# PSUM banks handed out one by one, and in-weight conversions moved behind batch 0, in a fused attention and MoE kernel

## The chip, the cores and the metric

The kernel runs on one core of a Trainium2 chip. The metric is the device time of one launch in microseconds (us). The core's engines are PE (TensorE, the matrix engine), DVE (VectorE), ACT (ScalarE), POOL (GpSimd) and SP (SyncE), which here only issues transfers (DMA). Each engine works through its own instructions in order. PSUM, the memory that PE writes, has eight banks of 512 floats for each of 128 partitions.

## The reference, cut to what matters

Attention with a band below the row's maximum, for 8 batches, 8 heads, 576 tokens, head size 64; then a gated two-layer unit on the 4608 tokens of width 512, with an inner width of 1536:

```python
scores = scale * np.matmul(q, k.transpose(0, 1, 3, 2))
thresh = np.max(scores, axis=-1, keepdims=True) - tau
scores = np.where(scores >= thresh, scores, -1000000000.0)
attn = np.exp(scores - np.max(scores, axis=-1, keepdims=True))
attn = attn / (np.sum(attn, axis=-1, keepdims=True) + 1e-09)
x = np.matmul(attn, v)          # heads side by side: 4608 x 512
gate = 1.0 / (1.0 + np.exp(-(x @ w_gate)))
out = (gate * (x @ w_val)) @ w_out
```

The weights come in as 64-bit floats, which the kernel receives as pairs of 32-bit words.

## The kernel before, in words

**Attention** goes by *visits*: one batch and one pair of heads, 32 visits in all, four to a batch. A visit has nine score tiles: four of each head (128 queries against all 576 keys), and one of the leftover 64 queries of both heads. A score tile `s` takes two PSUM banks. PE fills it (lines 591 for the first four visits, 599 later); DVE takes each row's maximum (606); POOL or DVE works out the threshold (615); ACT takes the exponential into `p` (620); DVE masks and sums it (623), and with that the score tile is free. DVE inverts the sum (655), POOL scales `p` by it (657), PE transposes it in four pieces into one bank, `tp` (668), ACT copies that to `pt` (630); the leftover keys go the same way, `lk` to `pl` (681). Two tiles of both heads are then multiplied with the values into one bank, `av` (704), and ACT copies the result to `xf`. For the first blocks `xf` is split into a high and a low float half, `x` (714 on ACT, 716 on POOL).

**The MoE** follows batch by batch. A *unit* of the in-product is 12 matmuls of 512 columns into one bank `m` (764): 24 units to a batch (12 column blocks, gate and value), then the out-product `o` (807). The last six batches and the leftover tokens go in pairs through seven products instead of eight (1006 and 1071), with sums of weights worked out earlier on POOL.

**The weights** have to be converted from 64-bit floats once. A conversion loads the raw words (`wr`), takes an exponent part on POOL (424, `wa`) and ACT (428, `wb`, which holds a PSUM bank), joins words on DVE (431, 437), and makes a high half on ACT (449) and a low half on POOL (455) or DVE (451) into `ws`. `ws` is stored to DRAM (`wid` for gate and value, `wod` for out) and loaded again by later batches. The first `OWN` in-weights are also used by batch 0 from where they are made; the other in-weights batch 0 loads back (`wi_6_0a` and so on).

**What sets the order.** The program first lists all operations with their engine, a cost, a key and their dependences. A planner then plays them through in time: whenever an engine is free it starts the operation with the lowest key whose inputs are ready and whose buffers have room, and this order is what is issued. Keys are counted in score tiles: visit after visit takes nine. MoE matmuls have keys above all others on PE, so they fill what attention leaves. `CONV_IN` and `CONV_OUT` give the key of the first conversion and the step to the next; `SHIFT` is the gap between the keys of batch 0 and batch 1; `LAG` is what the planner allows between an operation's end and the start of one that depends on it on another engine; `SLOTS` counts the buffers of each kind. PSUM is two score tiles (tag `s`) and four single banks (tag `b`), each tag a pool that gives its buffers in turn. Of the four banks conversions may hold one, attention three (two once the MoE has begun), the MoE two, and all four after the last attention output.

## Time and profile before

| | |
|---|---|
| median of 3 runs | 1355.14 us (1352.18 to 1357.49) |
| span of the profiled execution | 1352.1 us, no time of its own is given beside it |
| PE / DVE / ACT / POOL busy | 98 / 71 / 54 / 47% |
| mean granted PE clock | 0.992 |
| moved by DMA | 317.83 MB, mean 235 GB/s |

The profile is of one execution. A row of a group reads: line, engine, operation, written and read tiles with shapes, count, then busy time and mean nanoseconds of one, then the engine's idle time just before those instructions and what ended it. A row of the waits reads: who waited for whom, us in total, times, the longest. A row of a timeline: start, duration, engine, line. "PEld" is PE's weight loads, "PEclk" the granted clock.

The page's row of 40 equal slices shows PE at 7 to 8 tenths in the first three slices (of 33.8 us) and at 9 or more from then to the last but one.

### The profile page before, as it was taken

What the parts mean: (1) busy time and instruction counts of PE and PEld (TensorE: products, weight loads), DVE (VectorE), ACT (ScalarE), POOL (GpSimd) and SP (SyncE); (2) the same over time, 40 slices, a digit from 0 to 9 for tenths busy, and PEclk for the clock granted to TensorE, in tenths of its full rate; (3) what the DMA queues carried; (4) which work ended last, traced back from release to release, by engine and by line L of the source; (5) the groups of instructions that cost most, each with busy time, mean ns of one, the idle gap of its engine ahead of it and who ended that gap; (6) DMA issues with size and microseconds to landing.
All of it is one profiled execution on the core that took longest, in us unless ns stands there. A gap on an engine that the chain in (4) does not pass through costs nothing.

```text
span 1352.1 us, 23686 instructions
## 1 busy us (share of the span) xinstructions
PE 1320.8 (98%) x8292; PEld 1084.1 (80%) x8292; DVE 954.8 (71%) x1943; ACT 726.9 (54%) x1339; POOL 630.3 (47%) x660
## 2 busy tenths in 40 slices
PE   7879999999999999999999999999999999999998
PEld 4557888888888888888888878888888888888887
DVE  7889868567877777778787763556965569654594
ACT  7878766666766766667776653223532225322242
POOL 6985957956777764967776741101000110001100
PEclk8989999999999999999999999999999999999999
DMA  9879999897978988898897858656695656756564
GB/s 341 279 251 309 311 257 269 233 279 209 264 212 242 261 242 227 250 267 238 238 270 188 241 179 295 205 180 211 201 308 183 201 193 204 249 180 204 186 221 129
DMA packets 140436, 317.83 MB, mean 235 GB/s; under 512 B 22048, under 2 KB 49952, under 8 KB 140320
## 3 DMA queue, kind: packets, MB, share of 16 engines
q1 hardware_dynamic: 140176, 316.33, 76.5%
q8 instruction: 67, 1.10, 0.4%
q14 instruction: 49, 0.40, 0.1%
q10 hardware_dynamic: 144, 0.00, 0.0%
HBM read 210.37 MB, written 54.53 MB: 196 GB/s over the span
## 4 chain that ended last, share of the span: by engine, by line
PE 87%; DMA 6%; DVE 2%; ACT 2%; issue 1%; POOL 1%; SPq 1%; ACTq 0%; DVEq 0%; POOLq 0%
PE m L764 13%; PE qb L1006 11%; PE av L704 11%; PE s L599 8%; PE qc L1006 7%; PE qa L1006 7%; PE tp L668 7%; PE o L807 6%; PE rb L1071 5%; PE rc L1071 4%; PE ra L1071 4%; DMA wo<-wod 2%; DMA kd<-k 2%; PE s_l L599 1%; PE lk L681 1%
## 5 line engine op out<-in xcount | busy, mean ns | idle before, releaser
L657 POOL TENSOR_SCALAR p<-p,zero_t,sm 128x576 f32<-128x576 f32 x256 | 216.3, 856 | 107.9 <-DVE sm L655 76.5
L606 DVE TENSOR_REDUCE st<-s 128x1 f32<-128x576 f32 x256 | 192.3, 754 | 91.9 <-PE s L599 83.2
L623 DVE SCALAR_TENSOR_TENSOR p<-s,st,p 128x576 f32<-128x576 f32 x256 | 205.9, 812 | 30.2 <-ACT p L620 23.9
L620 ACT ACTIVATE p<-s,st 128x576 f32<-128x576 f32 x256 | 190.2, 750 | 57.4 <-DVE st L606 56.5
L919 POOL TENSOR_TENSOR gA<-gA 128x512 f32<-128x512 f32 x18 | 24.1, 1341 | 416.2 <-DVE gA L985 416.2
L630 ACT COPY pt<-tp 128x512 f32<-128x512 f32 x256 | 147.4, 589 | 54.0 <-PE tp L668 51.9
L599 PE MATMUL s<-kd,qd 128*128 128x288 f32 x896 | 165.0, 308 | 3.7 <-issue 1.6
L668 PE MATMUL tp<-ident,p 128*128 128x128 f32 x1024 | 156.7, 282 | 2.5 <-POOL p L657 2.0
L764 PE MATMUL m<-x,wi 128*128 128x512 f32 x576 | 158.9, 403 | 0.0
L668 PEld LDWEIGHTS tp<-ident,p 128*128 128x128 f32 x1024 | 123.2, 143 | 29.4 <-POOL p L657 7.6
L599 PEld LDWEIGHTS s<-kd,qd 128*128 128x128 f32 x896 | 133.9, 190 | 14.6 <-DVE p_l L623 2.4
L704 PE MATMUL av<-pt,vs 128*64 128x256 f32 x1024 | 126.1, 389 | 0.0
L807 PE MATMUL o<-g,wo 128*128 128x512 f32 x432 | 117.5, 401 | 0.0
L943 DVE TENSOR_TENSOR qu<-qb,qp 128x512 f32<-128x512 f32 x72 | 49.8, 692 | 89.9 <-PE qb L1006 77.1
L764 PEld LDWEIGHTS m<-x,wi 128*128 128x128 f32 x576 | 99.9, 189 | 14.3
L1006 PE MATMUL qa<-xs_p,wa 128*128 128x512 f32 x432 | 109.6, 389 | 0.0
L704 PEld LDWEIGHTS av<-pt,vs 128*64 128x64 f32 x1024 | 68.6, 138 | 48.5 <-issue 7.5
L1006 PEld LDWEIGHTS qa<-xs_p,wa 128*128 128x128 f32 x432 | 81.1, 188 | 16.8
L807 PEld LDWEIGHTS o<-g,wo 128*128 128x128 f32 x432 | 75.5, 189 | 10.9
L630 ACT COPY xf<-av 128x256 f32<-128x256 f32 x64 | 25.6, 399 | 77.4 <-PE av L704 73.1
L911 ACT CAST gs_p<-gA 128x512 fp32r<-128x512 f32 x54 | 32.4, 620 | 64.5 <-DVE gA L985 26.5
L981 ACT ACTIVATE gA<-qa 128x512 f32<-128x512 f32 x18 | 10.8, 598 | 103.4 <-PE qa L1006 103.4
(148 smaller groups left out, 2628.3 us busy)
## 6 DMA issues: line engine op xcount, KB each, us to landing
kd<-k SPq DMA_DIRECT2D x112, 320.0 KB, 6.0
wi<-wid SPq DMA_DIRECT2D x48, 512.0 KB, 6.9
wo<-wod SPq DMA_DIRECT2D x36, 512.0 KB, 7.0
wa<-wid SPq DMA_DIRECT2D x36, 512.0 KB, 4.1
ws<-sid SPq DMA_DIRECT2D x36, 512.0 KB, 4.5
wt<-sid SPq DMA_DIRECT2D x36, 512.0 KB, 3.3
wo_p<-sod SPq DMA_DIRECT2D x36, 512.0 KB, 4.6
qd<-q SPq DMA_DIRECT2D x112, 128.0 KB, 4.6
```

Source lines behind the costliest of these rows:

```text
L599: nc.tensor.matmul(s.ap[:, c, :HALF], st(), mv(slice(kc + c * HALF, kc + (c + 1) * HALF)), start=m == 0, stop=m == len(steps) - 1,)
L606: op("DVE", 0.76, key, lambda: nc.vector.tensor_reduce(out=st.ap[:, 0:1], in_=sv(), axis=AX.XY, op=ALU.max, negate=True), reads=[s], write ...
L620: op("ACT", 0.74, key, lambda: nc.scalar.activation(p(), sv(), AF.Exp, bias=st.ap[:, 0:1], scale=1.0), reads=[s, (st, 0)], writes=[(g.p, i)])
L623: op("DVE", 0.9, key, lambda: nc.vector.scalar_tensor_tensor(out=p(), in0=sv(), scalar=st.ap[:, 1:2], in1=p(), op0=ALU.is_ge, op1=ALU.mult ...
L630: return op("ACT", act(n), key, lambda: nc.scalar.copy(dst(), src.ap), reads=[src], writes=[part])
L657: op("POOL", 0.9, key, lambda i=i: nc.gpsimd.tensor_scalar(out=p.ap[:, i * S : (i + 1) * S], in0=p.ap[:, i * S : (i + 1) * S], scalar1=zer ...
L668: nc.tensor.matmul(tp.ap[:, c, :], self.p.ap[:, o + c * P : o + (c + 1) * P], ident, is_transpose=True, start=c == 0, stop=c == NJ - 1, sk ...
L704: nc.tensor.matmul(av.ap[h * D : (h + 1) * D, a:z], vis.vs.ap[:, j, h], m(h), start=i == 0, stop=i == len(ms) - 1, skip_group_check=True,)
L764: nc.tensor.matmul(m.ap, wv[:, a, c * P : (c + 1) * P], xs[c].ap[:, z, c0:c1], start=e == 0, stop=e == 11,)
L807: nc.tensor.matmul(acc.ap, wv[:, f, a], g[fg * ND + f].ap[:, z], start=(fg, f, a, z) == (0, 0, 0, 0), stop=(fg, f, a, z) == (NFG - 1, ND - ...
L1006: nc.tensor.matmul(acc.ap, wv[:, y, (2 * h + c) * P : (2 * h + c + 1) * P], xt[prod][c].get()[:, z], start=e == 0 and prod in FIRST, stop= ...
L1071: nc.tensor.matmul(acc.ap, w.ap[:, e, c, y], gt[prod][2 * g + c].get()[:, z], start=m == 0 and g == 0 and prod in FIRST, stop=m == 5 and g ...
```

## The change

PSUM is no longer two rotating pools. For each `s` and `b` tile the planner now settles a *place* when the tile is given out: score tiles may take banks 0-1, 2-3 and, until the first MoE product is issued, 4-5; single banks are 6 and 7, and after that point also 4 and 5. Each place is a pool of its own with one buffer, so a tile waits only for the last user of its banks. Ahead of the first product there are thus three score tiles, and two banks for all else. With it go other numbers: in-conversions start at key 36 with a step of 2 (from 10 and 1.5), which is behind batch 0's attention; `OWN` is 24, so batch 0 loads no in-weight back; batch 1's keys start 35 behind batch 0 (50 before); POOL works out the thresholds of the first visit of batch 1 too; six low halves go from DVE to POOL; PE's lag is 1.0 instead of 1.2; there is one more buffer of `p`, `x` and `w`; and a visit's scores may not start before a given MoE unit has ended (three units to a visit, from the sixth visit on).

```diff
     def make(self, b):
+        if b.place is not None:
+            at = min(b.place)
+            tag = f"{b.tag}{at}"
+            return self.bank_pool(tag).tile(b.shape, b.dtype, tag=tag, name=b.name, bufs=1)
         pool, bufs = self.pools[b.tag]
...
+        if not self.settle([b for s in need.values() for b in s]):
+            return False
...
+    def settle(self, bufs):
+        taken = set().union(*self.live.values()) if self.live else set()
+        places = {}
+        for b in bufs:
+            if b.tag not in ("s", "b"):
+                continue
+            for at in self.homes(b.tag):
+                if not taken & at:
+                    places[b] = at
+                    taken |= at
+                    break
+            else:
+                return False
...
-    "p": 3, "pc": 1, "sm": 8, "st": 16, "pt": 2, "pl": 2, "ptc": 1, "plc": 1, "xf": 2, "x": 5, "g": 12,
-    "w": 8, "t2": 6,
+    "p": 4, "pc": 1, "sm": 8, "st": 16, "pt": 2, "pl": 2, "ptc": 1, "plc": 1, "xf": 2, "x": 6, "g": 12,
+    "w": 9, "t2": 6,
-CONV_IN, CONV_OUT = (10, 1.5), (56, 3)
+CONV_IN, CONV_OUT = (36, 2), (56, 3)
-THR_FIRST, THR_UNTIL, LK_UNTIL = "POOL", 36, 300
+THR_FIRST, THR_UNTIL, LK_UNTIL = "POOL", 72, 300
-OWN = 12
-SHIFT = 50
+OWN = 24
+SHIFT = 35
-DVE_LO_IN, DVE_LO_OUT = range(18,24), ()
-LAG = {"PE": 1.2, "DVE": 0.3, "ACT": 0.08, "POOL": 0.3, "SP": 0.08}
+DVE_LO_IN, DVE_LO_OUT = (), ()
+LAG = {"PE": 1.0, "DVE": 0.3, "ACT": 0.08, "POOL": 0.3, "SP": 0.08}
+RATE, SLACK = 3, 3
...
-    pools["s"], pools["b"] = (ps, 2), (ps, 4)
+    pools["s"], pools["b"] = (ps, 3), (ps, 4)
...
         def cap(self, tag, cls):
+            if tag == "s" and active["moe"]:
+                return 2 if cls is None else None
...
+        def homes(self, tag):
+            if tag == "s":
+                return [{0, 1}, {2, 3}] + ([] if active["moe"] else [{4, 5}])
+            return [{6}, {7}] + ([{4}, {5}] if active["moe"] else [])
...
+    def held_by(vis):
+        n = RATE * (4 * vis.b + vis.hp - 4) - SLACK
+        return [unit_ends[n]] if RATE and 0 <= n < len(unit_ends) else []
...
-    nc = _bacc.Bacc("TRN2", target_bir_lowering=False, num_devices=1)
+    nc = _bacc.Bacc("TRN2", target_bir_lowering=False, num_devices=1, dynamic_dma_scratch_size=2048)
```

How instructions move, at three places. Line numbers of the changed program are larger (591 is 638 there, 606 is 653, 623 is 670, 431 is 478, 437 is 484, 668 is 719). In names such as `s_0_020` the first number is the visit's pair, then the head and tile; `l` is the tile of the leftover queries.

PE at the start of the program, before:

```order
L591 MATMUL s_0_000_196<-kp_0_0_174,qp_0_176 128x288 x2
L591 MATMUL s_0_001_204<-kp_0_0_174,qp_0_176 128x288 x2
L591 MATMUL s_0_l_228<-kp_0_0_174,qp_0_176 64x288 x2
L591 MATMUL s_0_l_228<-kp_0_1_180,qp_0_176 64x288 x2
L591 MATMUL s_0_020_235<-kp_0_0_174,qp_0_176 128x288 x2
L668 MATMUL tp_0_000_251<-ident,p_0_00_215 128x128 x4
```

and in the change:

```order
L638 MATMUL s_0_000_199<-kp_0_0_177,qp_0_179 128x288 x2
L638 MATMUL s_0_001_205<-kp_0_0_177,qp_0_179 128x288 x2
L638 MATMUL s_0_020_214<-kp_0_0_177,qp_0_179 128x288 x2
L638 MATMUL s_0_l_241<-kp_0_0_177,qp_0_179 64x288 x2
L638 MATMUL s_0_l_241<-kp_0_1_183,qp_0_179 64x288 x2
L638 MATMUL s_0_021_248<-kp_0_0_177,qp_0_179 128x288 x2
L638 MATMUL s_0_100_258<-kp_0_1_183,qp_0_179 128x288 x2
L719 MATMUL tp_0_000_269<-ident,p_0_00_219 128x128 x4
```

Six score tiles now stand ahead of the first transpose, where four did.

DVE in the second visit of batch 0, before:

```order
L606 TENSOR_REDUCE st_1_100_595<-s_1_100_582 128x1
L623 SCALAR_TENSOR_TENSOR p_1_02_536,sm_1_02_552<-s_1_021_569,st_1_021_588,p_1_02_536 128x576
L655 RECIPROCAL sm_1_02_552<-sm_1_02_552 128x2
L623 SCALAR_TENSOR_TENSOR p_1_10_614,sm_1_10_626<-s_1_100_582,st_1_100_595,p_1_10_614 128x576
L606 TENSOR_REDUCE st_1_101_632<-s_1_101_618 128x1
L431 SCALAR_TENSOR_TENSOR wb_0_624<-wb_0_624,wa_0_478 128x512
L606 TENSOR_REDUCE st_1_120_644<-s_1_120_629 128x1
L437 SCALAR_TENSOR_TENSOR wa_0_478<-wr_0_362,wb_0_624 128x512
L623 SCALAR_TENSOR_TENSOR p_1_10_614,sm_1_10_626<-s_1_101_618,st_1_101_632,p_1_10_614 128x576
```

and in the change, from the same tile on:

```order
L653 TENSOR_REDUCE st_1_100_519<-s_1_100_487 128x1
L653 TENSOR_REDUCE st_1_101_527<-s_1_101_500 128x1
L653 TENSOR_REDUCE st_1_120_555<-s_1_120_521 128x1
L670 SCALAR_TENSOR_TENSOR p_1_10_529,sm_1_10_560<-s_1_100_487,st_1_100_519,p_1_10_529 128x576
L670 SCALAR_TENSOR_TENSOR p_1_10_529,sm_1_10_560<-s_1_101_500,st_1_101_527,p_1_10_529 128x576
L706 RECIPROCAL sm_1_10_560<-sm_1_10_560 128x2
L670 SCALAR_TENSOR_TENSOR p_1_12_563,sm_1_12_574<-s_1_120_521,st_1_120_555,p_1_12_563 128x576
L653 TENSOR_REDUCE st_1_121_587<-s_1_121_567 128x1
L484 SCALAR_TENSOR_TENSOR wa_1_351<-wr_1_208,wb_1_471 128x512
```

Three maxima now follow one another, and fewer conversion steps (431 and 437, now 478 and 484) stand between: up to the last masked sum of batch 0 there are 7 pairs of them where there were 18.

SP around the store that ends batch 0's last visit (`xp_3`), before:

```order
L460 DMA wid_1_120<-ws_1_1398 128x1024
L1177 DMA xp_3_139<-xf_3_1325 256x1x32
L535 DMA kd_1_0_1434<-k_1_1357 64x2x640 x2
L531 DMA qd_1_1_1441<-q_1_1385 64x512 x2
L416 DMA wr_2_1453<-in_moe_w_out_dram 128x1024
L535 DMA kd_1_1_1462<-k_1_1357 64x2x640 x2
L504 DMA kn_2_1472<-in_k_dram 128x640
L498 DMA vs_2_1477<-in_v_dram 128x768
L460 DMA wid_0_121<-ws_0_1460 128x1024
```

and in the change:

```order
L1228 DMA xp_3_142<-xf_3_1243 256x1x32
L578 DMA qd_1_1_1314<-q_1_1264 64x512
L582 DMA kd_1_1_1347<-k_1_1233 64x2x640
L507 DMA wid_1_113<-ws_1_1312 128x1024
L582 DMA kd_1_1_1347<-k_1_1233 64x2x640
L557 DMA qn_2_1360<-in_q_dram 128x640
L545 DMA vs_2_1366<-in_v_dram 128x768
L463 DMA wr_2_1371<-in_moe_w_out_dram 128x1024
L461 DMA wr_0_1402<-in_moe_w_gate_dram 128x1024
L507 DMA wid_0_114<-ws_0_1394 128x1024
L511 DMA wod_128<-ws_2_1404 512x1x256
L463 DMA wr_2_1490<-in_moe_w_out_dram 128x1024
```

Behind batch 0 SP now still has raw in-weights (`in_moe_w_gate_dram`, `in_moe_w_val_dram`) to load between those of the next visits; before, they had been issued by then. The twelve reloads of in-weights for batch 0 (`wi_6_0a` to `wi_11_1a`) are gone from SP's order further on. On every engine the other counts are as before, but for 10 copies of leftover keys (DVE to ACT) and 9 thresholds (DVE to POOL).

More of the change, by code (lines that the diff above doesn't have):

```diff
@@ L29, in __init__ @@
         self.plan, self.tag, self.shape, self.dtype, self.name, self.cls = plan, tag, shape, dtype, name, cls
-        self.t, self.accesses, self.users, self.held = None, [], 0, False
+        self.t, self.accesses, self.users, self.held, self.place = None, [], 0, False, None
         self.turn = plan.made[tag] = plan.made.get(tag, 0) + 1
@@ L52, in __init__ @@
         self.ops, self.held, self.made, self.given = [], {}, {}, {}
+        self.live = {}
     def buf(self, tag, shape, dtype, name, cls=None):
@@ L117, in cap @@
         return None
+    def settle(self, bufs):
[11 more added lines that the diff above has]
+                return False
+        for b, at in places.items():
+            b.place = self.live[b] = at
+        return True
     def run(self):
@@ L179, in run @@
                         if not b.users and b.held:
+                            self.live.pop(b, None)
                             self.held[b.tag] -= 1
@@ L353 @@
     nc.vector.tensor_scalar(out=scale_t, in0=tau_t, scalar1=0.0, scalar2=QSCALE, op0=ALU.is_ge, op1=ALU.mult)
-    warm = ps.tile([P, 2, SM], F32, tag="s", name="warm")
+    ahead = ExitStack()
+    ps_more = ahead.enter_context(tc.tile_pool(name="ps_more", bufs=1, space=PSUM))
+    warm = ps.tile([P, 2, SM], F32, tag="s0", name="warm", bufs=1)
     for i in range(WARM):
@@ L375, in cap, with bank_pool @@
             return 2 if active["att"] else 4
+        def homes(self, tag):
+            if tag == "s":
+                return [{0, 1}, {2, 3}] + ([] if active["moe"] else [{4, 5}])
+            return [{6}, {7}] + ([{4}, {5}] if active["moe"] else [])
+        def bank_pool(self, tag):
+            if tag == "s4":
+                return more[0]
+            if tag in ("b4", "b5"):
+                if more[0] is ps_more:
+                    ahead.close()
+                    more[0] = ctx.enter_context(tc.tile_pool(name="ps_late", bufs=1, space=PSUM))
+                return more[0]
+            return ps
         def started(self, o):
@@ L381, in started @@
                 active["att"] = 0
-    last_att = [None]
+    last_att, more = [None], [ps_more]
     plan = Both(pools, slots)
@@ L602, in scores @@
                     )
-        op("PE", 0.8 if vis.plain_s else len(steps) * 2 * mm(HALF), key, plain_scores if vis.plain_s else scores, reads=reads, writes=[s], also=[g.p])
+        op("PE", 0.8 if vis.plain_s else len(steps) * 2 * mm(HALF), key, plain_scores if vis.plain_s else scores, reads=reads, writes=[s], also=[g.p], after=held_by(vis))
         st = buf("st", [P, 2], F32, f"st{n}")
```

## The prediction

> **What bounds it now.** I read the page first, then the stretches, then what DVE and PE do ahead of the first MoE product.
>
> ```profile
> span 1352.1 us, 23686 instructions
> PE 1320.8 (98%) x8292; PEld 1084.1 (80%) x8292; DVE 954.8 (71%) x1943; ACT 726.9 (54%) x1339; POOL 630.3 (47%) x660
> ```
>
> PE is busy for 1320.8 of 1352.1 us, and the order of the change holds the same number of PE matmuls of each line, so what a change can move is the 31.3 us in which PE is idle, and the speed at which it runs. The first product of the MoE starts at 108.72 us:
>
> ```profile
> 108.72 2.11 PE L764 MATMUL m<-x,ws 128*128 128x512 f32 x8
> ```
>
> The stretches cut there and at the ends of the later stages (us, then PE, PE loads, DVE, ACT, POOL, granted clock, DMA share, GB/s):
>
> ```profile
> core 0: us, PE busy (x) PEld busy (x) DVE busy (x) ACT busy (x) POOL busy (x), PEclk, DMA share, GB/s
> 0.00:108.70 108.70, 86.59 (x643) 57.65 (x643) 92.11 (x191) 84.98 (x163) 87.62 (x125) 0.91 0.84 287
> 108.70:240.00 131.30, 129.34 (x857) 106.77 (x859) 104.52 (x233) 90.68 (x170) 91.97 (x91) 1.00 0.98 287
> 240.00:800.00 560.00, 557.11 (x4321) 467.10 (x4318) 417.35 (x1007) 377.24 (x707) 389.37 (x401) 1.00 0.84 239
> 800.00:1352.00 552.00, 547.74 (x2476) 452.64 (x2473) 340.83 (x514) 174.00 (x300) 61.35 (x46) 1.00 0.63 208
> ```
>
> Of the idle time, 22.1 us lie ahead of the first product, 2.0 and 2.9 in the two mixed stretches, 4.3 in the last. So this case is about the first 108.7 us, in which batch 0's attention runs with no product to fill PE's gaps, and about whether what is won there is kept in the next 131 us, where DMA is busy for 0.98 of the time.
>
> Who sets the pace of the first stretch? DVE's first maximum starts at 6.59 us, and the last of its masked sums for batch 0 at 96.05:
>
> ```profile
> 6.59 1.42 DVE L606 TENSOR_REDUCE st<-s 128x1 f32<-128x576 f32 x2 [2.47 <-PE s L591]
> 96.05 0.81 DVE L623 SCALAR_TENSOR_TENSOR p<-s,st,p 128x576 f32<-128x576 f32 x1
> 6.59:96.90 90.31, 70.04 (x517) 44.24 (x516) 80.91 (x164) 71.84 (x138) 77.78 (x110) 0.90 0.89 306
> ```
>
> Thus 36 score tiles take 90.31 us, 2.51 us each. With two score tiles each is held for about 5.0 us: PE fills it, DVE takes the maximum, ACT the exponential, DVE the masked sum. In these 90.31 us DVE is idle for 9.4, POOL for 12.5, ACT for 18.5, PE for 20.3. DVE is the fullest, and the waits (first 97 us) show a loop between it and PE:
>
> ```profile
> PE s L591 <- DVE p L623: 13.0, 12, 2.4
> POOL st L615 <- DVE st L606: 7.3, 4, 6.2
> DVE st L606 <- PE s L591: 4.7, 6, 2.5
> DVE p L623 <- ACT p L620: 2.3, 4, 1.0
> ```
>
> PE waits 13.0 us for DVE to leave a score tile; DVE then waits 4.7 us for the next scores.
>
> **The change part by part.** DVE's groups up to 97 us:
>
> ```profile
> L623 DVE SCALAR_TENSOR_TENSOR p<-s,st,p 128x576 f32<-128x576 f32 x32 | 25.8, 814 | 4.9 <-ACT p L620 2.3 <-POOL st L615 2.0 <-POOL ws L455 0.4
> L606 DVE TENSOR_REDUCE st<-s 128x1 f32<-128x576 f32 x33 | 24.2, 751 | 4.9 <-PE s L591 4.7
> L431 DVE SCALAR_TENSOR_TENSOR wb<-wb,wa 128x512 int32<-128x512 int32 x18 | 12.4, 690 | 0.4 <-ACT wb L428 0.2
> L437 DVE SCALAR_TENSOR_TENSOR wa<-wr,wb 128x512 int32<-128x512 int32 x18 | 12.3, 684 | 0.3
> ```
>
> *Conversions behind batch 0.* Ahead of the last masked sum of batch 0, DVE's order held 18 pairs of conversion steps and now holds 7. Eleven pairs at 0.690 + 0.684 us are 15.1 us less; two maxima of batch 1 that now stand ahead add 2 x 0.751 = 1.5; net -13.6. DVE's groups in that stretch add up to some 89.9 us against 81.3 busy up to there (its instructions overlap at their ends), a factor of 0.905: **-12.3 us**. POOL loses 10 first steps and 9 low halves there, about 20 us by the rows below, ACT some 11, so DVE stays the fullest.
>
> *Three score tiles.* Three in flight at 5.0 us would allow 1.67 us a tile, below the 1.9 us (68.6/36) that DVE then needs, so the loop through PE should no longer set the pace. Bounds: nothing, to the 4.9 us idle ahead of the maxima. I take **-3**.
>
> *Two banks for everything else.* Until the first product, transposes, leftover keys, attention outputs and a conversion share two banks instead of four. The nearest rows:
>
> ```profile
> 101.00 1.09 PE L668 MATMUL tp<-ident,p 128*128 128x128 f32 x8
> 101.79 1.09 ACT L630 COPY pt<-tp 128x512 f32<-128x512 f32 x2
> L630 ACT COPY pl<-lk 128x128 f32<-128x128 f32 x16 | 4.6, 287 | 0.0
> 136.70 1.95 PE L704 MATMUL av<-pt,vs 128*64 128x256 f32 x16
> ```
>
> A transpose group fills its bank for 0.55 us and is copied in 0.55 to 0.6; with a quarter of a microsecond for each handover (the first group ends near 101.55, its copy starts at 101.79) it holds a bank for some 1.65 us. Nine of those, five leftover keys (about 1.1) and two outputs (about 3.5) make 27 bank-us a visit, 109 for four; seven conversions at some 4 us (ACT's 0.66, DVE's 1.37 and the waits between) add 28. That is 137 over two banks, 69 us of the 77 that the stretch should take: it fits, but tightly. While a conversion holds one bank (28 us) the rest must pass through the other, at 109/77 = 1.4 times what one bank can do, which costs up to 10 us. Bounds 0 to +10; the average load is below 1, so **+2**.
>
> *From the last masked sum to the first product.* This took 11.8 us (96.9 to 108.7). The two transposes now stand ahead of an attention output, and POOL's order between them holds more work (a 1.7 us key half, conversions): 0 to +3, I take **+1**. PE has one more group of batch 1's scores (four matmuls) behind it by then: **-0.5**.
>
> *The mixed stretch.* Fourteen in-conversions are still to come, and six low halves go from DVE to POOL.
>
> ```profile
> L455 POOL TENSOR_TENSOR ws<-wa,ws 128x512 fp32r<-128x512 f32 x16 | 20.5, 1281 | 3.9 <-DVE st L606 2.1 <-ACT ws L449 1.8
> L424 POOL TENSOR_SCALAR wa<-wr,zero_t 128x512 f32<-128x512 f32 x23 | 18.8, 818 | 3.0 <-DMA wr<-in_moe_w_gate_dram 1.7 <-DMA wr<-in_moe_w_val_dram 1.1
> L657 POOL TENSOR_SCALAR p<-p,zero_t,sm 128x576 f32<-128x576 f32 x34 | 28.3, 843 | 6.0 <-DVE sm L655 6.0
> 114.08 3.65 PE m L764 x16
> ```
>
> Between the last x half and the weights of the sixteenth unit, POOL has 15 low halves, 11 first steps, 10 normalisations and some eight others, about 48 us by these rows. PE has 180 product matmuls (0.228 us each) and the attention between them, about 65 us, before it needs those weights. The margin is 17 us, so the weights should not be late. DMA is tighter:
>
> ```profile
> DMA packets 18564, 37.96 MB, mean 288 GB/s; under 512 B 2651, under 2 KB 8795, under 8 KB 18552
> q1 hardware_dynamic: 18552, 37.81, 97.1%
> wi_0a<-wid SPq DMA_DIRECT2D x6, 512.0 KB, 8.7
> wi_1a<-wid SPq DMA_DIRECT2D x6, 512.0 KB, 8.8
> ```
>
> (108.7 to 240 us.) Twelve reloads of 0.52 MB go, 6.3 MB or 22 us of DMA time at 288 GB/s. Counting SP's order with the sizes of the transfers, 33.2 MB stood ahead of the store that ends batch 0's last visit, and 25.1 do now; 66.3 MB ahead of the first out-weight load, and 58.4 now. Every later mark is reached with 3 to 9 MB less, so 12 us sooner is affordable overall, but the moved loads fall into the first 40 us of the mixed stretch, while the reloads that go lay behind that. PE's lead time in the planner's table falls from 1.2 to 1.0 us, which can leave an in-order wait where there was slack; banks given out by which is free, not by turn, can take one away. Bounds: the 4.9 us of idle time won, to 9 us lost (worked out below). I take **+1**. The pacing of later visits by MoE units leaves PE's matmuls as they were; by the last visit 1200 product matmuls stand ahead of it, against 1224. The last 552 us are unchanged.
>
> *Sum:* -12.3 - 3 + 2 + 1 - 0.5 + 1 = -11.8. The profiled execution's span of 1352.1 becomes 1340.3. The runs' median, 1355.14, is 3.0 above that span, which I add: **1343 us**. The first product should start near 96 us.
>
> PE's clock gives another measure. These eight transposes took 1.97 us, against 1.09 at 101.00:
>
> ```profile
> 11.07 1.97 PE L668 MATMUL tp<-ident,p 128*128 128x128 f32 x8
> ```
>
> At a mean clock of 0.90 about a tenth of PE's 70.04 busy us, 7 us, is lost to the low clock. It is not in the sum, since DVE sets the pace; it belongs to the low end. The Trainium skill ("TensorE: Matmul & The Clock Gate", HAM oscillation) lets the clock fall after idle gaps of about 3.4 us; here it falls although the longest PE waits listed are 2.4 us, so the trace does not bear out that limit for single waits.
>
> **The rivals.**
>
> *More than that.* PE stays at full clock, the 4.9 us ahead of the maxima go, and so do the mixed stretches' 4.9: -12.3 - 4.9 + 0 + 0 - 0.5 - 4.9 = -22.6, 1333 us. For it: a single releaser, the score tile, stands ahead of PE's largest wait. Against: two banks.
>
> *The drains take over.* The third score tile buys nothing because transposes now queue for two banks, and each maximum comes as late as before. Then the tiles keep their 2.51 us, DVE merely idles where conversions were, and the first product stays near 105 to 109 us: 1351 to 1356, no change. For it: 137 bank-us at 88% of two banks. Against: those 10 us need every conversion to fall on a crowded moment. The example kernel of the Trainium skill ("TensorE: Matmul & The Clock Gate", HAM oscillation) gained nothing from double-buffering PSUM once PE was kept busy; here PE is idle for 20.3 of these 90.31 us, so the trace speaks against carrying that over.
>
> *DMA makes the mixed stretch slower.* From the store of the last visit of batch 0 to that of the next visit, SP's order now has 15.4 MB (10.3 before), while PE needs 35 us as before plus 38 more product matmuls at 0.24, 44 in all. That is 350 GB/s against the 288 that 97% busy engines moved; at 288 it takes 53 us, and keys and raw weights come 9 us late, which leaves 1352. It decides the sign when the rate falls under 15.4 MB in 56 us, 275 GB/s; at 240 GB/s it is 20 us late and the time 1363. Against: the stretch ahead carries 8.1 MB less and was at 0.84, so loads can run ahead, and PE has in-order products between the score rows.
>
> That the change does not do what it says can be left out: PE's order shows three score tiles filled ahead of the first masked sum.
>
> **How the numbers follow.** Forecast 0.57, more 0.14, drains 0.19, DMA 0.10. All of "more" and nearly all of the forecast (whose own range is 1336 to 1349, with drains and mixed stretch each some 3 us either way and DVE's waits from 0 to 4.9) is faster by over 0.5%, that is under 1348.4, about what a measurement of this kernel can tell from no change: 0.70. Drains, the forecast's upper edge and the milder half of the DMA case are within 0.5%: 0.22. The rest, above 1361.9, is slower: 0.08. The range runs from the "more" case to the upper end of the drains, 1333 to 1355.
>
> **What would show it.** Right: the first product between 92 and 100 us; DVE's last masked sum of batch 0 near 84; PE's wait for DVE at the scores well under 13.0 us; granted clock above 0.91 up to there; PE idle in the 130 us behind it still near 2 us. Wrong: PE waiting at transposes for ACT's copies (drains), or PE idle at scores behind key transfers, or at products behind conversions, soon after the first product (DMA).

## The result and the profile after

| | before | after |
|---|---|---|
| median of 20 runs each | 1355.53 us (1349.91 to 1360.24) | 1348.28 us (1344.10 to 1354.24) |
| ratio to before, 95% interval | | 0.9947 (0.9933 to 0.9961) |
| span of the profiled execution | 1352.1 us | 1342.9 us |
| mean granted PE clock | 0.992 | 0.999 |
| first MoE product at | 108.72 us | 96.79 us |

The change is 7.25 us faster by the medians, 9.2 by the two profiled spans. A launch takes 1.8 us more than its span in each run of both kernels, so the profiled execution of the change (1344.7 us with that) was a quick one among its twenty, 3.6 below their median, and that of before was 1.6 below its own.

The head of the page after the change:

```profile
span 1342.9 us, 23617 instructions
PE 1316.9 (98%) x8292; PEld 1078.1 (80%) x8292; DVE 952.0 (71%) x1918; ACT 732.9 (55%) x1349; POOL 639.6 (48%) x675
```

The first product in PE's timeline, and the last masked sum of batch 0 in DVE's:

```profile
96.79 4.61 PE L815 MATMUL m<-x,ws 128*128 128x512 f32 x12 [0.75 <-ACT pl L677]
80.12 0.81 DVE L670 SCALAR_TENSOR_TENSOR p<-s,st,p 128x576 f32<-128x576 f32 x1
```

The stretches after the change: from DVE's first maximum to the end of that sum, from there to the first product, from there to 230 us, and the whole opening (us, then PE, PE loads, DVE, ACT, POOL, clock, DMA share, GB/s):

```profile
6.08:80.93 74.85, 62.82 (x513) 38.53 (x509) 66.18 (x144) 61.41 (x116) 60.09 (x93) 1.00 0.73 242
80.93:96.79 15.86, 13.00 (x115) 9.32 (x114) 11.91 (x23) 15.13 (x29) 14.43 (x17) 1.00 0.75 223
96.79:230.00 133.21, 129.77 (x870) 106.03 (x871) 106.69 (x226) 97.12 (x181) 107.32 (x109) 0.99 0.92 289
0.00:96.79 96.79, 80.42 (x647) 51.92 (x647) 78.37 (x169) 78.99 (x149) 75.22 (x115) 1.00 0.73 235
```

The 36 score tiles of batch 0 take 74.85 us where they took 90.31, and the tail behind them 15.86 where it took 11.86 (96.86 to 108.72). PE's idle time ahead of the first product falls from 22.1 to 16.4 us, and its busy time there from 86.6 to 80.4, for 643 and 647 instructions: its clock is 1.00 where it was 0.91. Over the whole span PE is idle for 26.0 us instead of 31.3 and busy for 1316.9 instead of 1320.8: of the 9.2 us, 5.3 are idle time and 3.9 the same matmuls done in less time.

PE's waits in the first 97 us (us in total, times, longest):

```profile
PE lk L732 <- ACT pt L677: 3.5, 5, 0.8
PE s_l L638 <- DVE p L670: 2.0, 1, 2.0
PE tp L719 <- ACT pt L677: 1.5, 1, 1.5
PE tp L719 <- ACT pl L677: 1.5, 3, 0.6
PE s L638 <- DVE p L670: 1.4, 2, 1.2
```

The 13.0 us for which PE waited for a score tile are down to 1.4, and 2.0 at a tile of leftovers. In their place stand waits at transposes and leftover keys for ACT's copies out of the two drain banks.

### The profile page after: what moved, and what is told of

It reads as the page before. It is cut to its first block, busy times and chain, and to the rows that moved or that the text cites. A ratio compares the mean times of both kernels' runs of the same rounds, so it can differ in the third digit from the quotient of the medians.

```text
span 1342.9 us, 23617 instructions
## 1 busy us (share of the span) xinstructions
PE 1316.9 (98%) x8292; PEld 1078.1 (80%) x8292; DVE 952.0 (71%) x1918; ACT 732.9 (55%) x1349; POOL 639.6 (48%) x675
## 4 chain that ended last, share of the span: by engine, by line
PE 88%; DMA 3%; POOL 2%; ACT 2%; DVE 1%; issue 1%; SPq 1%; POOLq 0%; DVEq 0%; ACTq 0%
PE m L815 14%; PE qb L1057 11%; PE av L755 10%; PE s L646 8%; PE tp L719 8%; PE qc L1057 7%; PE qa L1057 7%; PE o L858 6%; PE rb L1122 5%; PE rc L1122 4%; PE ra L1122 4%; PE s_l L646 2%; DMA wr<-in_moe_w_out_dram 1%; PE lk L732 1%; DMA wo<-wod 1%
## 5 line engine op out<-in xcount | busy, mean ns | idle before, releaser
L646 PE MATMUL s<-kd,qd 128*128 128x288 f32 x896 | 161.3, 307 | 1.0 <-DVE p L670 0.7
L719 PE MATMUL tp<-ident,p 128*128 128x128 f32 x1024 | 153.1, 276 | 8.0 <-POOL p L708 2.6
L719 PEld LDWEIGHTS tp<-ident,p 128*128 128x128 f32 x1024 | 118.9, 140 | 38.8 <-issue 9.3
L815 PEld LDWEIGHTS m<-x,wi 128*128 128x128 f32 x576 | 99.3, 189 | 14.1 <-ACT pl L677 0.2
L815 PE MATMUL m<-x,ws 128*128 128x512 f32 x288 | 76.7, 406 | 1.2 <-ACT pl L677 0.8
```

The source lines that it names most:

```text
L646: nc.tensor.matmul(s.ap[:, c, :HALF], st(), mv(slice(kc + c * HALF, kc + (c + 1) * HALF)), start=m == 0, stop=m == len(steps) - 1,)
L719: nc.tensor.matmul(tp.ap[:, c, :], self.p.ap[:, o + c * P : o + (c + 1) * P], ident, is_transpose=True, start=c == 0, stop=c == NJ - 1, sk ...
L815: nc.tensor.matmul(m.ap, wv[:, a, c * P : (c + 1) * P], xs[c].ap[:, z, c0:c1], start=e == 0, stop=e == 11,)
```

## The experiments

Each is the changed kernel with one edit, except the eleventh. None leaves out a part of the computation. Four columns are read from their traces: the first product; PE's idle time from 97 to 230 and from 230 to 800 us (stretch less busy time); and the end of POOL's last low half of a weight, that is, when all weights are converted. Where the first product comes well behind 97 us (before, 1, 2, 10 and 11), the first idle column takes in the end of the opening. Each trace is one execution, and the executions of one kernel spread over some 10 us, so differences of two or three microseconds in the idle columns carry little.

| | ratio to before | median us | first product | idle 97–230 | idle 230–800 | weights done |
|---|---|---|---|---|---|---|
| before | 1 | 1355.5 | 108.7 | 2.3 | 2.9 | 224.0 |
| the change | 0.9947 (0.9933 to 0.9961) | 1348.3 | 96.8 | 3.4 | 2.3 | 227.0 |
| 1 two score tiles | 1.0041 (1.0026 to 1.0057) | 1362.4 | 110.8 | 5.2 | 6.6 | 252.8 |
| 2 early conversions | 1.0339 (1.0317 to 1.0362) | 1402.5 | 133.7 | 17.0 | 18.1 | 333.3 |
| 3 scratch in SBUF | 1.0034 (1.0021 to 1.0046) | 1360.5 | 96.3 | 10.6 | 6.8 | 246.2 |
| 4 twelve weights kept | 1.0083 (1.0062 to 1.0105) | 1368.5 | 98.5 | 11.2 | 11.9 | 247.0 |
| 5 conversions held back | 0.9994 (0.9971 to 1.0017) | 1355.2 | 97.2 | 6.1 | 10.1 | 242.1 |
| 6 out-weights 8 keys later | 1.0067 (1.0039 to 1.0096) | 1364.5 | 97.6 | 3.9 | 16.9 | 266.6 |
| 7 PE lead 1.2 | 0.9909 (0.9882 to 0.9935) | 1343.9 | 99.0 | 3.8 | 2.5 | 224.7 |
| 8 no pacing | 0.9955 (0.9933 to 0.9977) | 1349.9 | 99.2 | 4.3 | 7.6 | 229.1 |
| 9 PE lead 0.8 | 0.9961 (0.9945 to 0.9977) | 1350.5 | 95.2 | 4.1 | 5.9 | 231.0 |
| 10 PE lead 1.4 | 1.0040 (1.0026 to 1.0055) | 1360.9 | 106.5 | 5.6 | 4.5 | 249.4 |
| 11 before, PE lead 1.0 | 1.0051 (1.0031 to 1.0072) | 1362.2 | 112.9 | 4.7 | 5.6 | 225.8 |
| 12 PE lead 1.1 | 0.9947 (0.9929 to 0.9965) | 1348.3 | 98.9 | 1.9 | 6.3 | 235.7 |

### 1 and 2: the two halves of the opening, one at a time

Two score tiles throughout, four banks for the rest, everything else as changed:

```diff
-    pools["s"], pools["b"] = (ps, 3), (ps, 4)
+    pools["s"], pools["b"] = (ps, 2), (ps, 4)
-                return [{0, 1}, {2, 3}] + ([] if active["moe"] else [{4, 5}])
-            return [{6}, {7}] + ([{4}, {5}] if active["moe"] else [])
+                return [{0, 1}, {2, 3}]
+            return [{6}, {7}, {4}, {5}]
```

> The change with two score tiles at any time (banks 0 to 3) and four single banks (4 to 7) at any time, still given out one by one; conversions keep the late keys. Theory A (the gain is work taken off DVE ahead of the first product, and it needs both the late keys and the third tile, because with two tiles the planner again finds gaps on DVE and fills them with conversions: 18 pairs ahead of the last masked sum of batch 0, against 7): first product at 105 to 109 us, DVE's last masked sum near 96, time 1353 to 1357. Theory B (late keys alone bring the gain, the third tile nothing): first product at 95 to 98 us, time 1346 to 1350.

PE's waits over the whole run, and the first 97 us, with two tiles:

```profile
PE s L638 <- DVE p L670: 11.5, 11, 2.4
```

```profile
0.00:97.00 97.00, 75.26 (x539) 49.04 (x539) 79.50 (x167) 74.86 (x140) 74.25 (x112) 0.90 0.86 287
```

The old loop is back: 11.5 us of waits for a score tile, a clock of 0.90, DVE's last masked sum at 96.85, the first product at 110.8. DVE's order has 18 pairs of conversion steps ahead of the last masked sum of batch 0 again, although the keys are late: while PE and DVE wait for each other, the planner fills the holes with conversions whatever their key. So the late keys move nothing without the third tile. The time is worse than expected, and the conversions end 28.8 us later than before (252.8 against 224.0); that this is the reason is not tested here.

The other half alone, three tiles and two banks with the old keys:

```diff
-CONV_IN, CONV_OUT = (36, 2), (56, 3)
+CONV_IN, CONV_OUT = (10, 1.5), (56, 3)
```

> The change with the in-conversions' keys of the kernel before (10 and 1.5). Three score tiles and two single banks ahead of the first product. 16 conversion pairs stand ahead of DVE's last masked sum of batch 0. Theory A: nine more pairs at 1.24 us put the last sum 11 us later, near 92, first product at 105 to 109 us, time 1354 to 1360. Rival C (the third tile alone, by cutting the waits at the scores): first product at 96 to 100 us, time within 2 us of the change's, 1346 to 1350.

PE's waits and DVE's last masked sum of batch 0, in the first 95 us:

```profile
PE s L638 <- DVE p L670: 3.0, 5, 1.1
93.77 0.81 DVE L670 SCALAR_TENSOR_TENSOR p<-s,st,p 128x576 f32<-128x576 f32 x1
```

The third tile takes PE's wait for a score tile from 13.0 to 3.0 us (2.8 more at tiles of leftovers), as rival C had it, but the last masked sum, expected near 92, comes only 2.3 us sooner than before (96.05), with 16 pairs of conversion steps ahead of it instead of 18. In the change, with 7 pairs, it comes at 80.12. So up to there it is the work on DVE that sets the pace, and the third tile counts because it lets that work be put off.

Behind that sum comes the surprise. PE's timeline after the attention of batch 0's last visit, then the one conversion under way, by its step on ACT and its next on DVE:

```profile
115.61 0.33 PE L732 MATMUL lk_l<-ident,p_l 128*128 128x128 f32 x1 [0.68 <-ACT pt_l L677]
116.39 0.63 PE L719 MATMUL tp<-ident,p 128*128 128x128 f32 x4 [0.45 <-POOL p L708]
117.78 1.09 PE L719 MATMUL tp<-ident,p 128*128 128x128 f32 x4 [0.77 <-ACT pt L677]
119.55 0.48 PE L732 MATMUL lk<-ident,p 128*128 128x128 f32 x1 [0.68 <-ACT pt L677]
```

```profile
89.38 0.65 ACT L475 ACTIVATE wb<-wr 128x512 f32<-128x512 f32 x1
145.27 0.70 DVE L478 SCALAR_TENSOR_TENSOR wb<-wb,wa 128x512 int32<-128x512 int32 x1
```

Here the drains do take over: one transpose at a time, each waiting for the copy of the one ahead, and the first product at 133.7. The last fence says why: a conversion is begun on ACT at 89.38 us, which takes one of the two banks, and is not taken up again before 145.27. From 90 to 140 us no engine does any step of a conversion, and all drains go through one bank. What held it is not seen directly. From the code: kept weights stay in their buffers (12 of kind `g` for the first 16) until a product has used them, so conversions that run ahead fill these buffers and stop; they go on at 140.85, 7 us after the first product. It cost 54 us against the change, where 6 to 12 were expected. The third tile and the late keys are one change: with the rest of the change in place, either without the other is slower than before.

### 3: conversions without a PSUM bank

```diff
-    "w": 9, "t2": 6,
+    "w": 9, "t2": 6, "bt": 1,
-PAD = 64
+PAD = 48
-        bt = buf("b", [P, DM], F32, f"wb{name}", "conv")
+        bt = buf("bt", [P, DM], F32, f"wb{name}")
```

> The change with the conversion's scratch in SBUF, so that no conversion holds one of the two banks that drain transposes (16 words of padding go to make room). Theory D (two drain banks, one of them held by conversions, cost the 2 us that the forecast put there, and some of the 15.9 us from DVE's last masked sum to the first product): first product 2 to 5 us earlier than in the change, 92 to 95, PE's waits at lk and tp for ACT's copies at half or less of their 3.5 + 1.5 us. Rival (the tail is set by ACT and POOL, which are full there with conversions): first product within 1 us of the change's 96.8, time within 2 us of 1348.

With both drain banks free for attention PE's waits at `lk` and `tp` for ACT's copy of `pt` fall to 1.7 and 0.7 us, the half that theory D named, but the first product comes only 0.5 us sooner. What the banks alone are worth there is not separated by this, because the edit also makes the conversion's own steps slower, and in the tail POOL is now busy without a break (15.85 us of 15.85). The conversion's steps with the scratch in SBUF, then in the change:

```profile
L484 DVE SCALAR_TENSOR_TENSOR wa<-wr,wb 128x512 int32<-128x512 int32 x36 | 40.9, 1136 | 1.0
L478 DVE SCALAR_TENSOR_TENSOR wb<-wb,wa 128x512 int32<-128x512 int32 x36 | 38.9, 1080 | 3.7 <-POOL wa L471 2.5 <-ACT wb L475 0.9 <-POOL g L839 0.2
```

```profile
L478 DVE SCALAR_TENSOR_TENSOR wb<-wb,wa 128x512 int32<-128x512 int32 x36 | 24.9, 693 | 5.2 <-ACT wb L475 3.8 <-POOL wa L471 1.3
L484 DVE SCALAR_TENSOR_TENSOR wa<-wr,wb 128x512 int32<-128x512 int32 x36 | 24.7, 687 | 1.1
```

One step of 687 to 693 ns takes 1080 to 1136, 30 us of DVE's time in all, and the weights are done 19 us later; the kernel as a whole loses 12 us against the change.

### 4: twelve in-weights kept, as before

```diff
-OWN = 24
+OWN = 12
```

> The change with 12 in-weights kept and 12 reloaded by batch 0, as before. Theory E (DMA is the tight resource of the mixed stretch, 92% busy there): 6.3 MB more, PE idle between the first product and 230 us grows from 3.4 by 2 to 6 us, time 1350 to 1354. Rival (the reloads are hidden): time 1347 to 1349, first product as in the change.

The direction was as expected, the size not. PE's timeline of the in-products around 205 us, with twelve reloads (`wi_0a`, `wi_1a`):

```profile
202.99 2.09 PE L815 MATMUL m<-x,wi_1a 128*128 128x512 f32 x8
...
225.12 0.62 PE L815 MATMUL m<-x,wi_0a 128*128 128x512 f32 x2
```

Between these two rows, for 20.0 us, PE has no MoE product, only attention: it is idle for 7.5 us of them, and its clock is 0.75. In the change no such hole between 97 and 420 us is longer than 6.2 us (in the kernel before: 6.0). A reload can only follow the store that follows the conversion; keeping the weights takes that way out. With the reloads back the change loses 20 us, more than the opening won.

### 5: no conversions in the tail

From the eighth in-weight on, no conversion begins until POOL begins the low half of batch 0's last `x`:

```diff
     def room(self, o):
+        if o in self.late and not self.freed:
+            return False
...
+            if o is x_low[0]:
+                self.freed = True
...
+        if i == 2 or 2 * f + i >= HOLD_FROM:
+            plan.late |= {first, second}
```

> Nothing is left out of the computation: from the eighth in-weight on, no conversion is begun until POOL begins the low half of batch 0's last x. In the changed kernel the tail from the last masked sum of batch 0 to the first product takes 15.9 us, and in it ACT is busy for 15.1 and POOL for 14.4, with some ten conversion steps on ACT (6.3 us) and nine on POOL (9 us). Theory T (these steps lengthen the tail): the tail is back near 12 us, the first product near 93, and the five conversions come behind it, where POOL's margin of 17 us ahead of the sixteenth unit's weights falls to about 7: PE's idle time from 97 to 230 us stays within 2 us of 3.4, the time is 1344 to 1346. Rival U (the tail is set by PE, two drain banks and the chain through scores, sums and transposes): first product within 1 us of 96.8, time 1347 to 1350. Rival V (the work is only put off, and is late behind the first product): first product near 93, but PE's idle time from 97 to 230 us rises by 3 us or more, time 1348 to 1355.

The end of the tail here, POOL's low half of the last `x` and then PE's timeline:

```profile
93.60 1.27 POOL L776 TENSOR_TENSOR x<-xf,x 128x512 fp32r<-128x512 f32 x1
```

```profile
94.57 0.63 PE L728 MATMUL tp_l<-ident,p_l 128*128 128x128 f32 x4 [0.46 <-ACT pl L686]
95.87 0.33 PE L741 MATMUL lk_l<-ident,p_l 128*128 128x128 f32 x1 [0.68 <-ACT pt_l L686]
96.76 0.63 PE L728 MATMUL tp<-ident,p 128*128 128x128 f32 x4 [0.56 <-ACT pl_l L686]
97.16 1.20 PE L826 MATMUL m<-x,ws 128*128 128x512 f32 x4
```

`x` is complete at 94.87 us, against 96.55 in the change, so the conversions did hold it up, by 1.7 us (2.9 counted from DVE's last masked sum, which here starts at 81.34). Yet the first product is no sooner: the planner put more of batch 1's attention ahead of it on PE, and that now waits in turn for the two banks. Theory T falls as to the first product, U is right there. What U did not foresee is a part of V: PE has a hole of 12.0 us without a product, from 164.8 us on, while weights are being converted (PE's rows of the in-product, and POOL's low halves meanwhile):

```profile
163.61 1.20 PE L826 MATMUL m<-x,ws 128*128 128x512 f32 x4 [0.20 <-ACT th L840]
...
176.82 1.17 PE L826 MATMUL m<-x,ws 128*128 128x512 f32 x4
```

```profile
168.74 1.28 POOL L511 TENSOR_TENSOR ws<-wa,ws 128x512 fp32r<-128x512 f32 x1 [3.41 <-ACT ws L505]
172.33 1.27 POOL L511 TENSOR_TENSOR ws<-wa,ws 128x512 fp32r<-128x512 f32 x1 [0.70 <-ACT ws L505]
```

The idle time from 97 to 230 us rises by 2.7 us, where V asked for 3. Which weight the product at 176.82 had to wait for the trace does not show: by SP's next stores (`wid` issued at 169.9, `wod` at 175.3) the first of the two rows makes an in-weight and the second an out-weight, and PE had attention ahead of the product in its order. In the hole PE is idle for 3.3 us, at a clock of 0.86.

### 6: the out-weights a little later

```diff
-CONV_IN, CONV_OUT = (36, 2), (56, 3)
+CONV_IN, CONV_OUT = (36, 2), (64, 3)
```

> The out-weight conversions' due time is 64 + 3 each in place of 56 + 3, one edit. In the changed kernel POOL waits 9.7 us for raw out weights over the whole run, and PE's one long stall behind the first product, 2.2 us at 177, lies behind such a wait of 4.6 us. Theory M (out weights are asked for too early and take the place of in-weights in a full queue): the stall goes, PE's idle time from 97 to 230 us falls from 3.4 to about 1.5, time 1346. Rival (DMA is the bound there, and the waits only change their place): PE's idle time from 97 to 230 us stays between 2.5 and 4.5, time 1347 to 1351.

Both theories looked at the wrong place: up to 230 us nothing happens (3.9 us idle against 3.4). The loss of 16 us lies behind. PE's out-products (`o`), and POOL's last conversion:

```profile
252.01 3.92 PE L858 MATMUL o<-g,wo 128*128 128x512 f32 x12
...
289.21 0.63 PE L858 MATMUL o<-g,wo 128*128 128x512 f32 x2
```

```profile
249.31 0.79 POOL L471 TENSOR_SCALAR wa<-wr,zero_t 128x512 f32<-128x512 f32 x1 [3.96 <-DMA wr<-in_moe_w_out_dram]
...
261.51 0.79 POOL L471 TENSOR_SCALAR wa<-wr,zero_t 128x512 f32<-128x512 f32 x1
265.30 1.28 POOL L502 TENSOR_TENSOR ws<-wa,ws 128x512 fp32r<-128x512 f32 x1
```

From 255.9 to 289.2, 33.3 us, PE has no product. The third group of out-weights (the last four of twelve) is not complete before 266.6, and must then be stored and loaded again: SP issues the last store at 273.0 and the next loads of out-weights from 280.3 on. PE does not stand still meanwhile, it has attention to do. Its stretch reads (in the order given above):

```profile
255.93:289.21 33.28, 27.51 (x230) 22.30 (x230) 27.61 (x63) 22.08 (x43) 25.93 (x27) 0.90 0.96 291
```

So the hole itself costs 5.8 us of idle time and a tenth of the clock. Over the whole profiled span, 24.7 us longer than the change's, PE is idle for 14.3 us more and busy for 10.4 us more with the same 8292 matmuls; 7.0 us of its idle time lie between 400 and 800 us, where the change has 2.3. In the change POOL's last row reads:

```profile
225.74 1.30 POOL L502 TENSOR_TENSOR ws<-wa,ws 128x512 fp32r<-128x512 f32 x1
```

### 7, 9, 10, 11 and 12: the planner's lead time

```diff
-LAG = {"PE": 1.0, "DVE": 0.3, "ACT": 0.08, "POOL": 0.3, "SP": 0.08}
+LAG = {"PE": 1.2, "DVE": 0.3, "ACT": 0.08, "POOL": 0.3, "SP": 0.08}
```

and likewise 0.8, 1.1 and 1.4; and, in the kernel before, 1.0 in place of 1.2.

> The planner's lead time for PE is back at 1.2 us, everything else as in the changed kernel; the change's 11.8 us forecast gave it no term of its own. Theory L (the shorter lead puts PE's instructions where slack was, and costs the mixed stretch something): PE's idle time from 97 to 230 us falls from 3.4 to about 2, time 1346 to 1347. Rival (the lead time does not matter, the loads do): within 1 us of 3.4 there, first product within 1 us of 96.8, time 1347 to 1350.

> The planner's lead time for PE is 0.8 us in place of the change's 1.0 (1.2 measured 0.9909 of before, the change 0.9947). Theory O (what comes behind the first product hangs on which order the planner happens to fall into, and any small shift of one of its numbers moves the time by some 4 to 10 us either way, with the first 97 us much alike): first product within 3 us of 97, PE's idle time behind it anywhere from 8 to 25 us, time 1342 to 1358, in no order with the lead time. Rival (the lead time itself has a price, since PE waits in its order for what the planner thought ready): the time rises steadily as it is shortened, here 1351 to 1355, with the growth in PE's waits for ACT's copies, DVE's sums and POOL's products at transposes and keys.

> The planner's lead time for PE is 1.4 us in place of the change's 1.0. Theory O: first product within 3 us of 97, time 1342 to 1358, in no order with the lead time. Rival (longer is better): 1339 to 1343, PE's waits for ACT's copies, DVE's sums and POOL's products smaller than at 1.0.

> The kernel before with this one part of the change alone, the planner's lead time for PE at 1.0 us in place of 1.2. Theory O: first product within 3 us of 108.7, time anywhere within 8 us of 1355, more often worse than better, since the kernel before stands at 1.2. Rival (a shorter lead has a price of its own, 4 us in the change): 1358 to 1361, with PE's in-order waits grown.

> The planner's lead time for PE is 1.1 us, between the change's 1.0 (0.9947 of before) and 1.2 (0.9909); 0.8 gave 0.9961 and 1.4 gave 1.0040. Theory O (each value makes another order, and the time hangs on the order): anywhere from 1342 to 1361, not bound to lie between its neighbours. Rival (the time is a smooth function of the lead time with its best near 1.2): 1344 to 1348, first product between 96.8 and 99.0, PE's idle time from 97 to 800 us between 5.7 and 6.3.

At 0.8, 1.0, 1.1, 1.2 and 1.4 us the change measures 0.9961, 0.9947, 0.9947, 0.9909 and 1.0040. Neither "shorter costs" nor "longer helps" holds over the five. Nor does theory L: at 1.2 PE's idle time from 97 to 230 us is 3.8, not about 2, although the time is better than L expected. The kernel before loses 0.5% by one step of the number.

Theory O is not shown either. Its wide ranges hold at 0.8 and 1.1, but it misses the first product and the time at 1.4 (106.5 and 1360.9) and the first product of the kernel before at 1.0 (112.9). And the five times by themselves do not exclude the last rival, a smooth curve with its best near 1.2: at 1.1 it misses by 0.3 us in the time, and clearly only in the idle time (8.2 us from 97 to 800, where it asked for at most 6.3). What the traces show is two different things. The first product comes later with each step of the lead time: 95.2, 96.8, 98.9, 99.0, 106.5. What lies behind it follows no such order: the weights are done at 231.0, 227.0, 235.7, 224.7 and 249.4 us. Either way the same design is 4 us better or 13 us worse by this one number. At 1.4 the opening itself is lost, with both parts of the change in place (its clock in the first 97 us is 0.93). The variant at 1.2 is the fastest kernel measured, 1343.9 us; its interval overlaps that of the change by a hair (0.9935 against 0.9933), so that it beats before is shown, that it beats the change is not.

### 8: without the pacing of visits

```diff
-RATE, SLACK = 3, 3
+RATE, SLACK = 0, 3
```

> The pacing of later visits' scores by MoE units is taken out, everything else as in the changed kernel. My prediction costed the pacing at nothing. If that is right: first product within 0.5 us of 96.8, PE's idle time from 97 to 800 us within 1.5 us of 5.8, time 1346 to 1350. Rival (pacing spreads the attention, so that gaps of later visits stay filled): first product unchanged, PE's idle time from 230 to 800 us rises from 2.3 to 6 or more, time 1352 to 1358.

The time is within 0.1% of the change, so the pacing is worth about nothing, as it was costed. But the first product is 2.4 us later, which neither side had, and PE's idle time from 230 to 800 us is 5.3 us more, as the rival had it (steps of the lead time move it by up to 4.0, 2.3 to 6.3). This experiment decides little.

Four parts of the change were not tried alone: the gap of 35 between the keys of batch 0 and 1, the thresholds and the low halves moved to POOL, and the additional buffers.

### What the table shows together

Nine kernels have their first product between 95 and 99.3 us. In the order in which their weights are done (224.7, 227.0, 229.1, 231.0, 235.7, 242.1, 246.2, 247.0, 266.6 us) they measure 1343.9, 1348.3, 1349.9, 1350.5, 1348.3, 1355.2, 1360.5, 1368.5 and 1364.5. The time goes up with it, though not strictly. In experiment 6 the delay was put in by the edit itself, and the hole in PE's products stands in the trace where the weight is missing; there it is shown as a cause, if not as that of all 16 us. In experiment 5 the delay was put in too, but the trace does not tie the hole to one weight. For the others it is only seen to go together with the time.

## Why the prediction was right, and where it was wrong

The forecast was 1343 us, 12 less than before, and the range 1333 to 1355. It measures 1348.3: faster, in the range, with 7.25 of the 12 us. By the prediction's steps:

**What bounds it: right, with DVE ahead of the loop.** With two score tiles the loop between PE and DVE is back (experiment 1), and so are the conversions. With three and the old keys (experiment 2) the loop is nearly gone, yet DVE's last masked sum is only 2.3 us sooner: DVE, which the prediction called the fullest, sets the pace by its work.

**Conversions (-12.3) and third tile (-3): the sum right, its parts not.** The stretch shrinks by 15.46 us, forecast 15.3. But DVE's busy time there falls by 14.7 us (80.91 to 66.18) and not by 12.3, and its idle time by 0.7 (9.4 to 8.7), not by 3. DVE's groups up to its last sum show what changed:

```profile
L670 DVE SCALAR_TENSOR_TENSOR p<-s,st,p 128x576 f32<-128x576 f32 x32 | 25.6, 813 | 5.1 <-POOL st L662 4.3 <-ACT p L667 0.7
L653 DVE TENSOR_REDUCE st<-s 128x1 f32<-128x576 f32 x34 | 24.7, 747 | 3.6 <-PE s L638 3.6
L478 DVE SCALAR_TENSOR_TENSOR wb<-wb,wa 128x512 int32<-128x512 int32 x7 | 4.8, 689 | 0.4 <-ACT wb L475 0.4
```

The eleven pairs are gone as counted. The factor of 0.905 for overlapping ends was too low: the groups add up to 15.3 us less than before (89.0 to 73.7, from the start), the busy time to 14.7 less. And 1.35 us of this is nothing that the prediction counted, one step that prepares the queries of batch 1, before and after:

```profile
26.60 2.23 DVE L521 SCALAR_TENSOR_TENSOR q<-qn,scale_t,q 128x640 fp32r<-128x640 f32 x1
26.00 0.88 DVE L568 SCALAR_TENSOR_TENSOR q<-qn,scale_t,q 128x640 fp32r<-128x640 f32 x1
```

That the sum of the two terms came out within 0.2 us is luck: 2.4 us more on one side, 2.3 less on the other. Of the 4.9 us ahead of the maxima 3.6 stay, and 4.3 us now go to POOL's thresholds ahead of the masked sums (2.0 before). The two terms should also never have been two: experiment 1 shows that without the tile the conversions don't move, and experiment 2 that the tile by itself brings DVE 2.3 us at most.

**Two drain banks (+2): wrong place.** The stretch up to the last masked sum paid nothing for them. PE does wait for ACT's copies (3.5, 1.5 and 1.5 us above), but DVE, which sets the pace, is idle for 8.7 us there, no more than before (9.4). Experiment 2 shows the mechanism of the rival "the drains take over", but from a conversion that sits on a bank for 56 us, not from the average load of two banks that I had worked out.

**The tail (+1): mis-sized, it measured +4.0.** ACT is busy for 15.13 and POOL for 14.43 of its 15.86 us, seven conversion steps among them on ACT (4.5 us) and seven on POOL (8.2); experiment 5's expectation has ten and nine, which is the count only with the steps for `x` and for the next keys and queries. "POOL's order holds more work" was seen and priced too low. Experiment 5 says how much is theirs: 1.7 us at `x` (2.9 from the last masked sum), and nothing at the first product, where more of batch 1's attention and the two banks take their place. How the rest divides between banks and order stays open.

**The first product near 96: right,** at 96.79, and so the clock (1.00, was 0.91) and the fall of PE's waits. DVE's last masked sum came at 80.1 to 80.9, 3 us ahead of the forecast of 84, which the tail then took back.

**The mixed stretch (+1): mis-sized, 2.7 us are lost between the first product and the end** (11.9 us won there, 9.2 in the span). PE's busy time behind it is 2.3 us longer (1234.2 to 1236.5), its idle time 0.4 (9.2 to 9.6). Its clock is 0.99 up to 230 us, where it was 1.00.

**The rivals.** "DMA makes the mixed stretch slower" did not come about: the queue of the 130 us behind the first product moved 289 GB/s,

```profile
DMA packets 17662, 37.91 MB, mean 289 GB/s; under 512 B 2574, under 2 KB 8206, under 8 KB 17649
...
q1 hardware_dynamic: 17649, 37.75, 91.9%
```

at 91.9% instead of 97.1%. But the step beneath it, that only POOL's 17 us of margin ahead of the sixteenth unit mattered, looked at the in-weights alone. The out-weights have a limit of their own: done at 227.0 in the change, and when they come at 266.6 PE has no product for 33 us and the time is 16 us longer. "The weights should not be late" was true of this order by luck of its numbers, and the prediction had no term for the out-weights.

**The time around the span (+3.0).** The median after stands 5.4 us above its profiled span. Of that 1.8 us lie around the span in every run; the rest is that the profiled execution was a quick one. Together: +0.9 at the first product, +1.7 behind it and some +2.0 from the draws of the two profiled executions make up the missing 4.5 us (11.8 forecast, 7.25 measured).

## What to carry to other kernels

Where two engines hand a buffer back and forth and a planner starts whatever is ready, low-priority work flows into the holes whatever its priority says; more buffers and a later due time have to come together, and each has to be tried without the other before either is credited. When work is put off to shorten an opening, ask for each thing that it makes when its first consumer needs it, to the last one made: here out-weights that were done 40 us later, 170 us behind the stretch that was tuned, cost more than the opening had won. And when an order is planned from a table of numbers, move one number by a step and look at how far the time goes (here up to 13 us) before a gain of 7 us is put down to the design.

## What was not expected of the hardware

The same DVE step on 128 x 512 integers took 0.69 us with one input in PSUM and 1.08 to 1.14 us with both in SBUF (experiment 3), while POOL's steps grew too: low halves from 1302 to 1460 ns, first steps from 872 to 955. The Trainium skill ("SBUF — State Buffer", Who interferes with whom) says that a DVE instruction with two SBUF inputs contends with a GpSimd instruction that reads SBUF; this trace agrees, by 0.4 us an instruction. Of the 72 steps of experiment 3, the three during which POOL did nothing took 0.68 to 0.69 us, as with PSUM; the 63 during which POOL was busy nearly throughout took 1.10 on average and up to 1.77:

```profile
183.11 0.68 DVE L478 SCALAR_TENSOR_TENSOR wb<-wb,wa 128x512 int32<-128x512 int32 x1
146.51 1.77 DVE L478 SCALAR_TENSOR_TENSOR wb<-wb,wa 128x512 int32<-128x512 int32 x1 [0.17 <-POOL g L839]
```

So it is POOL's company, and not the place of the operand alone, that costs the time. The query step of 2.23 us above, which also has two SBUF inputs, began together with a POOL step of 1.55 us (`k<-kn,k`, at 26.60); where the two do not meet it took 0.88. A PSUM bank for scratch here also buys DVE time.

PE's clock fell far with short waits. From 100 to 130 us of experiment 2,

```profile
100.00:130.00 30.00, 20.80 (x145) 14.08 (x147) 9.88 (x24) 12.65 (x26) 9.27 (x15) 0.79 0.41 98
```

it is 0.79, and the longest wait listed there for PE is 0.8 us; in the opening before, it was 0.90 with waits of up to 2.4 us. The Trainium skill ("TensorE: Matmul & The Clock Gate", HAM oscillation) lets the clock fall after idle gaps of about 3.4 us; no listed wait in these stretches is that long. The busy share alone does not tell it either: in the first 97 us PE is busy for 80.62 in the change at a clock of 1.00, and for 80.17 with a lead of 1.4 at 0.93. What sets it stays open.
